# An FNet block with a gated MLP in fp32: the first product of the sequence transform made by seven smaller ones for two chunks at once, and operands of the MLP split in pairs

## The chip, the core and the metric

The kernel runs on one core of one Trainium2 chip. The metric is device time in microseconds (us), the median of three runs. Lower is better. Engines: PE is TensorE (matmul; PEld its weight loads), DVE is VectorE, ACT is ScalarE, POOL is GpSimd, SP issues most of the loads.

## The reference

`x` is 2048 x 512 in fp32. Cut to what matters:

```
xn = layernorm(x)                                  # 2048 x 512
a  = xn @ dft_hid_re.T ;  b = xn @ dft_hid_im.T    # transform along the hidden axis
s  = dft_seq_re @ a - dft_seq_im @ b               # transform along the sequence, 2048 x 2048
g  = silu( (sigmoid(xn @ w_gate) * (xn @ w_up)) @ w_down )   # 512 -> 1792 -> 512
out = x + s * g
```

## The kernel before, in words

**Arithmetic.** Every fp32 matmul is made of three. An operand is split into a high part, a copy rounded to `fp32r` by ACT, and a low part, the rest, subtracted by DVE (`split`, line 370). `mm3` (line 374) issues high x high, high x low and low x high into one PSUM bank. A tile in SBUF is called `page` whatever it holds, and a matmul is 128x128 weights by 512 columns unless a row says otherwise. PSUM has eight banks: `ga`, `ua`, `gb`, `ub`, `gc`, `uc` and two of `pd`.

**Three stages.** First the gated MLP: 14 blocks, two halves `h` of the sequence by seven groups `g` of 256 hidden columns. Then the sequence transform, which is done first of the two transforms and on `xn` itself: `dft_seq_re` and `dft_seq_im` times `xn`, in four chunks of 512 columns. Last the hidden transform, silu and the product. All three use the scheme of Strassen and Winograd: a 2 x 2 block product by seven block products instead of eight, named 1 to 7, of which four have sums or differences of blocks as operands. DVE makes these sums, in fp32, before the split.

**The sequence transform.** `Chunk` (line 1090) is one chunk of 512 output columns. Each of its products runs in four steps `pp` of 12 matmuls, so 48 matmuls a product. The first output block of a chunk is product 1 + product 2; the others build on product 1. Product 2 is not run by `Chunk`. `Inner` (line 1194) makes it for two chunks (`one`, `two`) together, with the scheme applied once more: seven inner products of 2 steps x 6 matmuls, 84 matmuls for both chunks. Its left operands (`inner_a`, line 1025) are made and split once while the MLP runs, stored to DRAM (`i_part`), and loaded again for each pair (`Kept`, line 1058). Its right operands (`inner_b`, line 1071) are loaded from `c_re`; four of seven are sums. `Inner.done` gives each finished bank to a chunk, and `Chunk.give` copies or adds it into the page `u1` that becomes the first output block. Product 1 seeds or stays in the banks `ga`/`ua` (`gb`/`ub` for chunks 2 and 3) in which products 6, 7 and 4 are then accumulated.

**The order of the work.** `PLAN` says for each chunk in which order its steps and those of `Inner` come (digits for `Chunk`, letters a to g for the inner products 1 to 7). Nothing is issued while the Python code runs through this: every call is recorded in `program`, and `emit` (line 319) issues the recorded instructions in the sequence of numbers in `ORDER`. Each engine then takes its own instructions strictly in that order; PE waits for a low part that DVE has not made yet, and DVE waits for a high part that ACT has not made. `HOMES` gives each new page its place in SBUF, so a load also waits for the last reader of that place.

**The MLP's operands.** `w_operands` (line 582) loads a block's weights and makes seven split operands of 128 x 512 (`Parts`, line 406). `Seven` (line 685) does the same for the seven operands of the down projection. Each is one ACT copy and one DVE subtraction. `BLOCKS` is the order of the 14 blocks; where two neighbours share a group `g`, the second uses the operands of the first again.

Of the kernel before, what the change touches and what calls it, by code (L numbers as in the profile page):

```python
# [9 lines left out]
F32 = mybir.dt.float32  # L10
# [5 lines left out]
P = 128  # L16
# [17 lines left out]
0-1 15 2 16 72 5 20 31 3-4 21 6 19 7 29 9 22 11 73 8 23 32 13 74 10 24 26 33 25 17 53 36 12 27 30 108 28 176  # L34
37 34 38 211 39 50 40 14 48 18 41-42 49 43 70 44 54 35 51 71 52 45 47 46 64 60 65 57 56 61-63 80 55 68-69 79
66 81 67 75-76 59 97-98 58 89 77-78 99 82 100 84 90 85 83 86-87 102 88 91 101 92 96 93-94 103 109-110 105
405 95 111-112 117 220 118-119 113 120 125 350 126 121 123-124 106 131 127-129 114 122 130 135 139 115 143
140-142 104 147 133 148 116 144 150-151 154 177 145-146 156-157 149 152 136 153 164 406 158 137 159-160 201
155 161-162 134 138 163 168 179 165 169 181 170 180 166 171-175 202 167 185-189 206 190 204 191-192 203
193-194 182 195 230 212 183 196 207-208 199 132 200 107 219 209-210 235 218 215-216 197-198 217 221 254 222  # L40
213-214 231 225-226 205 227-228 233 223-224 237-238 232 245 241 246 255 236 242 229 256 239-240 385 247 244
248 178 259 234 260 264 257-258 243 261-262 363 267 266 268-269 249 270 265 271-272 251 364 273-274 345
275-276 279 252 280 286-287 285 288-289 250 290-294 263 295 298-301 253 281-282 277 284 278 304 302 305 283
296-297 308 313-314 310 303 306-307 311 317-318 315 424 316 325 319 312 320 329-330 321-322 326-327 333-334
331-332 337 341 346 338 323 365 324 335-336 328 339 348 340 351-353 347 428 354-356 367 369-370 342 371-373
349 374-375 381 376-378 383 366 379-380 387-388 382 389 384 390 343 391-393 399 394 368 395-396 344 397-398
357 401 400 358-360 407 386 450 361 449 362 403 409 402 475 410-411 451 412 408 413 476 414-415 425 416 421
417-419 429 423 420 430 427 431 499 432-433 422 434-436 404 442 437-438 426 439 452 440-441 466 453-455 501
456 443 457-459 446 495 479-480 444 481 467 482 445 483 497 447 484-485 471 486 502 487-488 491 489-490 468
460 448 461-463 493 464 469 465 492 503-505 477 506 472 507-508 473 509 515 510-511 478 512-514 517 540 516  # L50
541 498 542 526 519 527 496 528 522 529-530 518 681 531 543 470 544 546 545 560 538 554 561-563 594 552
564-565 520 532 688 533-534 474 524 535-537 550 547 572 553 573 647 548 574-575 500 549 576-577 184 309 566
578 567-568 539 579 569-570 558 571 598 580 584-585 686 523 586 581 635 582 595 559 583 596 610 589 611 591
612 597 613 587 551 614 599 615 555 588 600 616-617 593 494 618 601 619-620 592 602 621 525 663 521 622
664-665 603 624 633 625-626 557 627-628 590 629 608 666-667 606 623 668 649-650 556 631 607 651-652 630 634
653-655 632 661 656-657 604 658 669 659-660 670 609 672-673 645 674 671 636 675 678 676 640 677 692 662 693
605 694 679 695-696 637 641 648 697 638 708 682 709 642 639 710 680 698 704 643 699-700 690 701 706 702-703
711 646 705 712-713 733 707 715 734-736 714 683 737-738 718 716 720 739-741 717 689 742-743 731 744 644 747
719 748 687 749-751 729 725 752 775 753 776 730 777 887 778 684 732 779 754 780 685 756 721 757 691 722 727
758-759 728 762 760 723 761 781 745 726 763 782-783 804 746 784 1004 764 785-786 768 787 765 788 755 789 766  # L60
773 790 772 791 769 792 815 797 816 793 774 817-818 794 819 767 820 795 770 823-824 799 825 771 826-827 805
828 798 832 801 830 833-835 829 796 836-837 821 831 806 809-810 822 811 803 812 807 813-814 800 857-859 839
808 860-861 847 862 851 838 852 802 853 849 854 840 855 961 856 842 928 865-866 863 867 848 868 891 869-870
844 871 893-894 874 895 864 896-897 872 878 898 909 905 910 875 841 911 876 912 882 913 850 873 914-915 899
843 900 885 901 724 902 907 916 903-904 918 888 877 906 919-921 1003 908 922-923 937 924 879 845 938 880 939
935 940 892 881 941 925 942-943 883 927 944-945 929 946 889 886 930 947-949 951 917 952-953 890 933 954 957
955 926 884 956 970 960 846 971 950 972 958 934 973-974 962 964 975 959 963 976 968 977-978 966 931 979 1010
980 932 981 999 982-983 936 984-985 988 986 965 987 990 989 967 991-992 1002 993 996 994 969 995 1023 1000
997 1024-1026 1021 1001 998 1027 1005 1028 1017 1037-1038 1036 1006 1039 1011 1007 1029-1030 1019 1031 1012
1032-1033 1022 1034 1043 1040-1041 1014 1042 1046 1044 1047 1018 1016 1048 1035 1049 1013 1050 1062 1051  # L70
1020 1066 1052 1015 1067-1068 1058 1069-1070 1055 1071 1053 1072-1073 1060 1054 1074-1075 1064 1056
1076-1077 1009 1080-1081 1078 1082 1059 1083 1008 1084 1079 1085 1092 1098 1086 1099-1100 1057 1096
1101-1102 1061 1103-1104 1110 1105 1063 1106 1045 1107 1087 1108 1065 1109 1088 1114 1111 1115-1117 1089
1120 1118-1119 1123 1121 1124 1090 1125 1137-1138 1129 1091 1139-1140 1094 1141 1093 1142 1209 1126-1127
1097 1128 1143 1095 1130 1144-1146 1112 1147-1149 1113 1132 1150-1151 1135 1152 1133 1153-1155 1166 1136
1167 1156 1168 1131 1169 1157 1170-1171 1162 1172 1122 1158 1173-1174 1164 1175 1159 1176 1163 1177
1180-1181 1160 1182 1165 1213 1186 1214-1215 1161 1216-1218 1178 1183-1184 1179 1185 1189 1187 1190 1199
1191 1134 1200 1192 1188 1195 1193 1207 1194 1219 1208 1196 1220-1222 1198 1197 1223-1224 1201 1230-1231
1225 1232 1202 1227 1211 1228 1203 1229 1244-1246 1204 1226 1247-1248 1266 1249 1205 1250-1251 1233 1206
1252-1253 1234 1254 1210 1255 1240 1256 1235 1257 1212 1269 1258 1237 1270 1259-1260 1242 1261 1277 1236  # L80
1265 1278-1279 1238 1280 1263 1281-1282 1243 1283 1262 1284-1285 1239 1267 1264 1286-1287 1271 1241
1288-1289 1273 1290 1268 1291-1292 1295 1293 1272 1294 1306 1274 1296 1307-1309 1275 1299 1310-1311
1320-1321 1302 1322 1276 1312 1298 1313-1314 1304 1315-1316 1300 1317-1318 1323-1324 1319 1325 1337 1303
1327 1338-1339 1301 1340 1326 1341-1342 1305 1343 1349 1344 1297 1345 1329 1346 1331 1347-1348 1353 1350
1354 1332 1355-1356 1359 1333 1357-1358 1369 1360 1370 1334 1371-1372 1367 1351 1373-1374 1335 1375-1377
1336 1378-1379 1330 1380-1382 1352 1383 1362 1384-1385 1361 1363 1386 1396 1388 1397 1364 1398-1399 1394
1400 1368 1401 1390 1402 1392 1403-1404 1366 1405-1407 1410-1411 1391 1412-1413 1416 1414 1395 1415 1431
1458 1408 1700 1432-1433 1427 1365 1434 1393 1435 1417 1409 1436-1437 1387 1438 1420 1439 1421 1440 1443
1389 1441-1442 1419 1445-1446 1328 1447 1422 1448 1451 1449-1450 1423 1462 1452 1463-1464 1425 1465 1429
1466-1467 1424 1468-1469 1483 1457 1470-1472 1455 1428 1473-1474 1444 1475 1454 1476 1460 1477 1430  # L90
1478-1479 1485 1493-1494 1481 1495 1456 1496 1480 1497-1498 1461 1487 1499-1501 1459 1489 1502-1503 1418
1514 1488 1504-1505 1518 1506 1486 1507 1453 1508 1491 1490 1509-1510 1522 1482 1523 1511 1492 1912
1524-1525 1512 1426 1526-1527 1520 1528 1515 1529 1484 1530-1534 1536 1516 1537-1539 1542 1540-1541 1519
1550 1548 1551 1517 1552 1535 1553-1554 1545 1521 1555-1556 1543 1557 1546 1558-1559 1562 1560 1547 1561
1566 1563 1567-1569 1549 1572 1570-1571 1664 1583 1579 1584-1585 1564 1586-1587 1513 1573 1588 1565 1699
1589 1574 1590 1575 1544 1591 1577 1592-1593 1576 1594-1595 1581 1596 1580 1597-1600 1604 1614 1582 1615
1601 1616-1619 1606 1622 1605 1623-1624 1608 1607 1628 1609-1613 1625 1620 1626-1627 1647 1632 1629 1648
1578 1649-1650 1602 1651-1652 1631 1603 1655 1621 1656 1634 1657 1641 1633 1642-1643 1635 1639 1644-1645
# [1434 lines left out]
```

## Time and profile before

| | |
|---|---|
| median of three runs | 795.08 us (794.29 to 796.54) |
| profiled execution, its device time | 795.25 us |
| span of its profile, first to last instruction | 793.4 us |
| matmuls, PE busy | 3512 (of 3514 issued), 785.5 us |
| DVE | 933 instructions, 716.4 us |
| ACT | 850 instructions, 540.8 us |
| DMA | 173.69 MB, mean 219 GB/s |

An engine's busy time is the time in which at least one of its instructions runs. Instructions of one engine overlap a little at their ends, so the pace of an engine is the distance from one start to the next, and not the duration that a row gives. The stages in the span: the MLP to about 401 us, the sequence transform to about 712 us, then the hidden transform; on DVE and ACT they overlap at the borders.

### The profile page before, as it was taken

What the parts mean: (1) busy time and instruction counts of PE and PEld (TensorE: products, weight loads), DVE (VectorE), ACT (ScalarE), POOL (GpSimd) and SP (SyncE); (2) the same over time, 40 slices, a digit from 0 to 9 for tenths busy, and PEclk for the clock granted to TensorE, in tenths of its full rate; (3) what the DMA queues carried; (4) which work ended last, traced back from release to release, by engine and by line L of the source; (5) the groups of instructions that cost most, each with busy time, mean ns of one, the idle gap of its engine ahead of it and who ended that gap; (6) DMA issues with size and microseconds to landing.
All of it is one profiled execution on the core that took longest, in us unless ns stands there. A gap on an engine that the chain in (4) does not pass through costs nothing.

```text
span 793.4 us, 10135 instructions
## 1 busy us (share of the span) xinstructions
PE 785.5 (99%) x3512; PEld 650.1 (82%) x3512; DVE 716.4 (90%) x933; ACT 540.8 (68%) x850; POOL 127.1 (16%) x174
## 2 busy tenths in 40 slices
PE   8999999999999999999999999999999999999997
PEld 7888887888888888888888888888888888888886
DVE  7999998899979988889898997999987899988986
ACT  5679998879867977877987756554544545457361
POOL 3002442212212322112110101010100000010102
PEclk9999999999999999999999999999999999999999
DMA  8223999969859899999998779359938479569427
GB/s 341 83 81 126 236 198 235 242 151 212 166 137 234 241 231 256 259 203 230 233 309 241 179 280 309 135 159 338 375 142 323 173 282 353 214 244 344 75 54 132
DMA packets 50035, 173.69 MB, mean 219 GB/s; under 512 B 5568, under 2 KB 5824, under 8 KB 49984
## 3 DMA queue, kind: packets, MB, share of 16 engines
q0 software_dynamic: 20160, 69.75, 40.0%
q1 hardware_dynamic: 29744, 103.23, 36.5%
q8 instruction: 27, 0.44, 0.2%
q14 instruction: 24, 0.20, 0.1%
q10 hardware_dynamic: 80, 0.07, 0.0%
HBM read 106.43 MB, written 70.27 MB: 223 GB/s over the span
## 4 chain that ended last, share of the span: by engine, by line
PE 95%; DMA 3%; DVE 1%; ACT 0%; POOL 0%; issue 0%; SPq 0%; DVEq 0%; ACTq 0%; POOLq 0%
PE pd L328 17%; PE ga L328 17%; PE ua L328 16%; PE gc L328 11%; PE uc L328 11%; PE gb L328 11%; PE ub L328 11%; DMA page<-in_w_gu_dram 2%; DMA g_part<-page 1%; DVE page L328 1%; ACT page L328 0%; POOL moments L328 0%; SPq L328 0%; POOL shifts L328 0%; DVE moments L328 0%
## 5 line engine op out<-in xcount | busy, mean ns | idle before, releaser
L328 DVE TENSOR_TENSOR page<-page 128x1024 fp32r<-128x1024 f32 (+5 forms) x756 | 629.5, 891 | 54.8 <-ACT page L328 45.3
L328 ACT ACTIVATE page<-page 128x512 fp32r<-128x512 f32 (+3 forms) x452 | 351.9, 824 | 138.5 <-DVE page L328 113.4
L328 PE MATMUL pd<-page 128*128 128x512 f32 x624 | 159.2, 390 | 0.3 <-ACT page L328 0.2
L328 PE MATMUL ga<-page 128*128 128x512 f32 (+1 forms) x606 | 156.5, 387 | 0.0
L328 PE MATMUL ua<-page 128*128 128x512 f32 (+1 forms) x594 | 154.0, 387 | 1.7 <-ACT page L328 1.7
L328 PEld LDWEIGHTS pd<-page 128*128 128x128 f32 x624 | 116.8, 188 | 25.6 <-ACT page L328 1.3
L328 PEld LDWEIGHTS ga<-page 128*128 128x128 f32 x606 | 113.1, 188 | 23.5 <-ACT page L328 0.2
L328 PEld LDWEIGHTS ua<-page 128*128 128x128 f32 x594 | 110.9, 188 | 24.8 <-ACT page L328 1.9
L328 POOL DMA_DIRECT2D g_part<-page x84 | 70.7, 887 | 316.0 <-ACT page L328 292.9
L328 ACT ACTIVATE page<-pd 128x512 f32<-128x512 f32 (+2 forms) x161 | 89.8, 576 | 38.7 <-PE pd L328 28.3
L328 PE MATMUL uc<-page 128*128 128x512 f32 (+1 forms) x420 | 110.1, 383 | 0.0
L328 PE MATMUL gc<-page 128*128 128x512 f32 (+1 forms) x420 | 109.9, 383 | 0.0
L328 PE MATMUL gb<-page 128*128 128x512 f32 (+1 forms) x420 | 109.0, 380 | 0.0
L328 PE MATMUL ub<-page 128*128 128x512 f32 (+1 forms) x396 | 105.5, 386 | 0.0
L328 PEld LDWEIGHTS uc<-page 128*128 128x128 f32 x420 | 78.0, 188 | 15.7 <-DVE page L328 0.2
L328 PEld LDWEIGHTS gc<-page 128*128 128x128 f32 x420 | 77.8, 188 | 15.7 <-ACT page L328 0.2
L328 PEld LDWEIGHTS gb<-page 128*128 128x128 f32 x420 | 76.9, 188 | 15.4 <-ACT gb L328 0.4
L328 PEld LDWEIGHTS ub<-page 128*128 128x128 f32 x396 | 73.7, 188 | 15.0 <-ACT ub L328 0.2
L328 ACT ACTIVATE page<-ga 128x512 f32<-128x512 f32 x51 | 30.5, 598 | 12.9 <-PE ga L328 12.8
L328 POOL DMA_DIRECT2D f_part<-page x16 | 8.7, 547 | 178.8 <-DVE page L328 165.6
L328 ACT ACTIVATE page<-gb 128x512 f32<-128x512 f32 x32 | 19.1, 598 | 20.0 <-PE gb L328 20.0
L328 ACT ACTIVATE page<-ua 128x512 f32<-128x512 f32 x36 | 21.6, 600 | 8.8 <-PE ua L328 8.3
(59 smaller groups left out, 245.5 us busy)
## 6 DMA issues: line engine op xcount, KB each, us to landing
g_part<-page POOLq DMA_DIRECT2D x84, 512.0 KB, 7.5
page<-in_c_re_dram SPq DMA_DIRECT2D x49, 512.0 KB, 5.9
page<-in_c_im_dram SPq DMA_DIRECT2D x33, 512.0 KB, 7.3
page<-in_w_gu_dram SPq DMA_DIRECT2D x26, 512.0 KB, 7.0
f_part<-page POOLq DMA_DIRECT2D x16, 512.0 KB, 7.6
page<-f_part SPq DMA_DIRECT2D x16, 512.0 KB, 5.4
page<-i_part SPq DMA_DIRECT2D x14, 512.0 KB, 5.1
page<-in_w_down_dram SPq DMA_DIRECT2D x13, 512.0 KB, 5.3
```

The source lines that it names most:

```text
L328: f(*map(found, a), **{n: found(v) for n, v in k.items()})
```

## The change

1. `Inner` now makes product 1 too, from the even blocks of 128 rows of `xn` and `c_re` (`j` = 0; product 2 takes the odd ones, `j` = 1). `PLAN` has capital letters for the inner products of product 1 and has no digits 1 or 2. Both go through `give` into `u1`; the banks of product 6 are seeded from `u1` (`Chunk.run`).
2. For this `inner_a`, `i_part`, `Kept` and `inner_b` exist twice.
3. `twins`: two operands that lie in one page are split by one ACT copy and one DVE subtraction of 128 x 1024 in the place of two of 128 x 512. The MLP's weights are split in three pairs and one single, the operands of the down projection too.
4. `BLOCKS` has the block (1, 5) moved behind (1, 6), so that two groups' weights are used by both halves without being loaded and made again; `shared` keeps them.
5. `ORDER` and `HOMES` are new as a whole.

The instructions that each program issues, counted by engine and shape (only the shapes whose number differs):

```
                                       before  after
PE   matmul 128x512 on pages             3360    3336     (ga -48, ua -48, ub -12, pd +84)
DVE  page<-page 128x1024                 328     427
DVE  page<-page 128x512                  352     191
DVE  page<-page 128x256                   76      94
DVE  page<-page and a bank, 128x512       28      32
ACT  page<-page 128x1024                 213     296
ACT  page<-page 128x512                  225      68
ACT  page<-page 128x256                   14      28
ACT  with a bank, 128x512 (those changed) 295    305
POOL store to i_part                       7      14
SP   load of i_part                       14      28
SP   load of c_re                         49      64
SP   load of w_gu and w_down              39      36
```

The core of the diff:

```diff
-BLOCKS = (*((0, g) for g in range(7)), (1, 6), *((1, g) for g in range(6)))
+BLOCKS = (*((0, g) for g in range(7)), (1, 6), (1, 5), *((1, g) for g in range(5)))
-0-1 15 2 16 72 5 20 31 3-4 21 6 19 7 29 9 22 11 73 8 23 32 13 74 10 24 26 33 25 17 53 36 12 27 30 108 28 176
...
+5565-5568 5572-5573 5569 5574-5579 5570 5580-5583 5571 5584-5587
...
+    def twins(loads, src, names, n):
+        def make():
+            v, pair = src(), (page([2, n]), page([2, n]))
+            split(*pair, v)
+            return pair
+        both = Value(loads, make)
+        return {k: Value(loads, lambda i=i: tuple(t[:, i] for t in both.get())) for i, k in enumerate(names)}
...
-        w = {k: Parts(loads, s, [4 * P], joint=True) for k, s in src.items()}
+        w = {
+            **twins(loads, loads[0].load, (1, 2), 4 * P),
+            **twins(loads, lambda: (s1.get(), s2.get(), two[0].get())[2], (5, 6), 4 * P),
+            **twins(loads, lambda: (s3.get(), s4.get(), two[1].get())[2], (7, 3), 4 * P),
+            4: Parts(loads, raw(1, 1), [4 * P], joint=True),
+        }
...
-            self.h = {k: Parts([], v, [SB], joint=True) for k, v in src.items()}
+            self.h = {
+                **twins([], lambda: (b11(), t1.get(), self.s[1])[2], (1, 5), SB),
+                **twins([], lambda: (b22(), t2.get(), self.s[3])[2], (3, 6), SB),
+                **twins([], lambda: (b21(), t4.get(), self.s[4])[2], (2, 4), SB),
+                7: Parts([], t3.get, [SB], joint=True),
+            }
...
     PLAN = (
-        "1111555566a6a633337777b4b444",
-        "e11e1f1f5c555c66663g3g777733d4d444",
-        "111155556666aa7777b44b44e333ef3f",
-        "1ccg1g1d1555d56666337777334444",
+        "AA5FFBB5GGEE5DDCC56666333377774444",
+        "5a5a5b5b66e66e33f33f77c77c4g44g4dd",
+        "AA5FFBB5GGEE5DDCC56666333377774444",
+        "5a5a5b5b66e66e33f33f77c77c4g44g4dd",
     )
...
             ch = CHAIN[k]
-            if k in FIRST and pp == 0:
+            if k in (5, 6) and pp == 0:
                 for d in range(2):
                     self.ps[ch, d] = bank("gu"[d] + (self.letter if ch == "a" else ch))
+                    if k == 6:
+                        nc.scalar.activation(self.ps[ch, d], self.s["u1"][:, d, :], AF.Copy)
...
-        inner_a([n + i for i in (-43, -39, -39, -38, -37, -33, -27, -20, -12, -10, 1)])
+        inner_a([n + i for i in range(-42, -20, 2)], 1)
+        inner_a([n + i for i in range(-41, -19, 2)], 0)
```

**PE where the sequence transform begins.** The rows below are PE's, in its order, `bank<-page` with the shape and how many follow one another; `pd`, and `gb`/`ub` before, are still the MLP's. Before, at the hand-over from product 1 of chunk 0 (banks `ga` and `ua`) to its product 5 (`gc` and `uc`):

```order
L328 MATMUL ga<-page 128x512 x3
L328 MATMUL ua<-page 128x512 x3
L328 MATMUL pd<-page 128x512 x6
L328 MATMUL gc<-page 128x512 x3
L328 MATMUL uc<-page 128x512 x3
```

Now, with the inner products in `gb` and `ub`, product 5 between them, and product 6 (`ga`) last:

```order
L331 MATMUL ub<-page 128x512 x12
L331 MATMUL gc<-page 128x512 x3
L331 MATMUL gb<-page 128x512 x12
L331 MATMUL gc<-page 128x512 x3
L331 MATMUL ub<-page 128x512 x12
L331 MATMUL uc<-page 128x512 x3
L331 MATMUL gc<-page 128x512 x3
L331 MATMUL pd<-page 128x512 x3
L331 MATMUL gc<-page 128x512 x3
L331 MATMUL uc<-page 128x512 x3
L331 MATMUL pd<-page 128x512 x3
L331 MATMUL ga<-page 128x512 x3
```

The 48 matmuls of product 1 are gone from `ga` and `ua`; 12 at a time stand in one bank instead, and 18 matmuls lie between the last of them and product 6.

**DVE in the second half of the sequence transform.** The rows are DVE's, in its order: `page<-page 128x1024` is a sum of two blocks or a low part, rows with a bank are results taken out of PSUM. Before, where chunk 1 ends and chunk 2 begins:

```order
L328 TENSOR_TENSOR page<-page 128x1024 x8
L328 TENSOR_TENSOR page<-ua,page 128x512
L328 TENSOR_TENSOR page<-ga,page 128x512
L328 TENSOR_TENSOR page<-page 128x1024 x3
L328 TENSOR_TENSOR page<-page,gc 128x512
L328 TENSOR_TENSOR page<-page 128x1024 x7
L328 TENSOR_TENSOR page<-page,gb 128x512
L328 TENSOR_TENSOR page<-page 128x1024 x4
L328 TENSOR_TENSOR page<-page,uc 128x512
L328 TENSOR_TENSOR page<-page 128x1024 x33
```

Now, in the same part of the program:

```order
L331 TENSOR_TENSOR page<-page 128x1024 x9
L331 TENSOR_TENSOR page<-page,pd 128x512
L331 TENSOR_TENSOR page<-page 128x1024 x33
L331 TENSOR_TENSOR page<-page,gc 128x512
L331 TENSOR_TENSOR page<-page 128x1024 x3
L331 TENSOR_TENSOR page<-page,uc 128x512
L331 TENSOR_TENSOR page<-gb,page 128x512
L331 TENSOR_TENSOR page<-ub,page 128x512
L331 TENSOR_TENSOR page<-page 128x1024 x7
L331 TENSOR_TENSOR page<-page,pd 128x512
L331 TENSOR_TENSOR page<-page 128x1024 x14
```

The kinds of work are the same; the stretches of wide instructions between two results are longer. Between the 2209th and the 2738th instruction of PE, 530 matmuls, a part that I call the dense stretch (in both programs it leads from chunk 1 into chunk 2), counted in the written order of all engines, the program before has 87 wide and 12 narrow instructions for DVE, 68 for ACT and 43 loads for SP; the changed one 101 wide and 11 narrow for DVE, 81 for ACT and 57 loads.

More of the change, by code (lines that the diff above doesn't have):

```diff
@@ L39 @@
[L39 to L43, printed above, removed]
@@ L984, in step @@
                 nc.gpsimd.dma_start(to, v)
-        for i, v in zip({diffs: (1, 3, 0, 0), sums: (0, 0, 3, 1)}[make], blocks):
+        for i, v in zip({diffs: (1, 3, 0, 0)}.get(make, (0, 0, 3, 1)), blocks):
             sooner(at[i] - ahead, v.load)
@@ L1069, in fnet_glu_kernel, with inner_b, behind @@
         get = load
-    def inner_b(pair):
+    def inner_b(pair, j):
         b = {}
         for i in range(2):
-            b11, b12, b21, b22 = (Load(c_re[c, 1, 2 * q + i], [2, SB]) for q in range(2) for c in pair)
-            t1 = Value([b11, b12], onto(b11.load, b12.load, SUB, nc.vector, True))
-            t3 = Value([b12, b22], onto(b12.load, b22.load, SUB, nc.vector, True))
-            t2 = Value([b22], onto(t1.get, b22.load, SUB, nc.vector, True))
-            t4 = Value([b21], onto(t2.get, b21.load, SUB, nc.vector, True))
+            b11, b12, b21, b22 = (Load(c_re[c, j, 2 * q + i], [2, SB]) for q in range(2) for c in pair)
+            def behind(k, i, make):
+                return lambda: (b[k, i].get(), make())[1]
+            t1 = Value([b11, b12], behind(1, i, onto(b11.load, b12.load, SUB, nc.vector, True)))
+            t3 = Value([b12, b22], lambda t1=t1, make=onto(b12.load, b22.load, SUB, nc.vector, True): (t1.get(), make())[1])
+            t2 = Value([b22], lambda t1=t1, b22=b22: combine(page([2, SB], F32), b22.load(), t1.get(), SUB))
+            t4 = Value([b21], behind(6, i, onto(t2.get, b21.load, SUB, nc.vector, True)))
             for k, v in {1: b11, 2: b21, 3: b22}.items():
@@ L1141, in done @@
         def done(self, k):
-            if k == 1:
-                if "2" not in PLAN[self.tc]:
-                    for d in range(2):
-                        self.give(d, self.ps["a", d])
-                else:
-                    for d in range(2):
-                        self.ps["b", d] = bank("gu"[d] + "ba"[self.letter == "b"])
-                        nc.scalar.activation(self.ps["b", d], self.ps["a", d], AF.Copy)
-            elif k == 2:
-                self.made[0] = self.snap("u1", "b")
-                self.put(0)
-            elif k == 5:
+            if k == 5:
                 self.snap("u5", "c")
@@ L1174, in run @@
                     ws = [t[:, o, d * P : (d + 1) * P] for t in wv]
-                    first = k in FIRST and pp == e == 0
-                    mm3(self.ps[ch, d], ws, [t[:, e, :] for t in xv], first, pp == 3 and e == 1, go_on=k not in FIRST)
+                    first = k == 5 and pp == e == 0
+                    mm3(self.ps[ch, d], ws, [t[:, e, :] for t in xv], first, pp == 3 and e == 1, go_on=k != 5)
             if pp == 3:
@@ L1420, in fnet_glu_kernel @@
     x_operands(1)
-    job = last = None
+    job, shared = None, {}
     ahead = []
     for h, g in BLOCKS:
-        made = g == last
+        made = h and g in shared
         if not made:
-            w, wd, last = w_operands(g), Down(g), g
+            shared[g] = w_operands(g), Down(g)
+        w, wd = shared[g]
+        if h or g < 5:
+            del shared[g]
         new = Seven(h, wd, made)
```

534 lines of the change are left out of this document (270 added, 264 removed).

## The prediction

> **What bounds the kernel now.** I read the page from the top: the busy times, the slices, then the chain that ended last.
>
> ```profile
> span 793.4 us, 10135 instructions
> PE 785.5 (99%) x3512; PEld 650.1 (82%) x3512; DVE 716.4 (90%) x933; ACT 540.8 (68%) x850; POOL 127.1 (16%) x174
> ...
> PE   8999999999999999999999999999999999999997
> ...
> DVE  7999998899979988889898997999987899988986
> ...
> PEclk9999999999999999999999999999999999999999
> ...
> PE 95%; DMA 3%; DVE 1%; ACT 0%; POOL 0%; issue 0%; SPq 0%; DVEq 0%; ACTq 0%; POOLq 0%
> ```
>
> The reader sees one engine that never rests: PE in every slice but the first and the last, at full clock, and 95% of the chain. DVE is second with 90%. So a matmul taken away is worth its whole pace, as long as nothing else makes PE wait. Next the stretches between fixed times (columns: time, PE, PEld, DVE, ACT and POOL busy with their instructions, clock, DMA share, GB/s), and all that PE waited for:
>
> ```profile
> 20.00:120.00 100.00, 100.00 (x451) 82.44 (x451) 98.55 (x160) 84.67 (x151) 25.28 (x33) 1.00 0.54 146
> 132.00:402.00 270.00, 269.79 (x1191) 222.86 (x1190) 243.95 (x384) 220.01 (x400) 55.85 (x72) 1.00 0.91 217
> 496.00:616.00 120.00, 120.00 (x531) 99.10 (x530) 108.79 (x100) 59.16 (x68) 8.23 (x13) 1.00 0.70 245
> 616.00:712.00 96.00, 96.00 (x425) 79.48 (x424) 87.04 (x82) 50.07 (x56) 4.42 (x8) 1.00 0.69 250
> 780.00:793.40 13.40, 9.03 (x52) 7.75 (x50) 7.78 (x12) 0.00 (x0) 2.95 (x3) 1.00 0.91 175
> ```
>
> ```profile
> PE ua L328 <- ACT page L328: 1.7, 1, 1.7
> PE gb L328 <- DVE page L328: 1.4, 1, 1.4
> PE pd L328 <- ACT page L328: 0.2, 1, 0.2
> ```
>
> Two things matter. From 20 to 120 us DVE was busy 98.55 of 100 us and PE lost nothing, so a nearly full DVE is not by itself a stall. And PE's idle time, 793.4 - 785.5 = 7.9 us, lies at the two ends (4.4 us in the last row, 3.1 us in the first two waits): there is nothing inside to win but matmuls.
>
> **The matmuls removed.** The chain in order of time (start, duration, what) gives the pace:
>
> ```profile
> 712.70 5.44 PE pd L328 x24
> 723.58 5.44 PE pd L328 x24
> ```
>
> 24 matmuls take 5.44 us, 0.2267 us each; the 390 ns that a row gives as one matmul's duration overlap with the next. Product 1 by `Chunk` is 48 matmuls, 96 for two chunks; by `Inner` 84. Two pairs save 2 x 12 = 24 matmuls of the same shape, 5.44 us of PE.
>
> **DVE's price.** DVE's rows in order of time (start, duration), where it does not rest:
>
> ```profile
> 62.37 0.68 DVE L328 TENSOR_TENSOR page<-page,uc 128x512 f32<-128x512 f32 x1
> 62.97 0.69 DVE L328 TENSOR_TENSOR page<-page 128x512 f32<-128x512 f32 x1
> 63.57 0.68 DVE L328 TENSOR_TENSOR page<-page,gc 128x512 f32<-128x512 f32 x1
> ...
> 399.21 1.23 DVE L328 TENSOR_TENSOR page<-page 128x1024 fp32r<-128x1024 f32 x1
> 400.36 0.68 DVE L328 TENSOR_TENSOR page<-page,ua 128x512 f32<-128x512 f32 x1
> 400.95 1.22 DVE L328 TENSOR_TENSOR page<-page 128x1024 fp32r<-128x1024 f32 x1
> 402.09 0.68 DVE L328 TENSOR_TENSOR page<-page,gc 128x512 f32<-128x512 f32 x1
> ```
>
> From start to start a narrow one (512) costs 0.60 us and a wide one (1024) 1.15 and 1.14; I take 1.14. For 128x256 I take the duration, as an upper end:
>
> ```profile
> L328 DVE TENSOR_TENSOR page<-page 128x256 f32<-128x256 f32 x62 | 25.3, 420 | 0.2
> L328 ACT ACTIVATE page<-page 128x1024 fp32r<-128x1024 f32 x205 | 209.9, 1056 | 125.7 <-DVE page L328 102.4 <-PE ub L328 6.9 <-issue 5.1
> L328 ACT ACTIVATE page<-page 128x512 fp32r<-128x512 f32 x197 | 118.5, 630 | 5.9 <-DVE page L328 4.1 <-DMA page<-in_w_gu_dram 1.8
> L328 ACT ACTIVATE page<-page 128x256 fp32r<-128x256 f32 x14 | 5.5, 419 | 0.0
> ```
>
> Over the program DVE gets 99 wide more (+112.9), 161 narrow fewer (-96.6), 18 of 256 more (+7.6) and 4 out of banks more (+2.4): +26.3 us, from 716.4 to about 743 in a span of about 790, 94%. ACT by the durations above: 83 x 1.056 - 157 x 0.63 + 14 x 0.42 + 10 x 0.63 (those with a bank) = +0.9 us. ACT has a third of the span free; its change is at nothing.
>
> It must be read by stage. Pairing saves 2 x 0.60 - 1.14 = 0.06 us of DVE a pair, and two groups fewer to make save their sums and splits; these lie in the MLP. The new operands of product 1 are DVE work in the sequence transform. In the dense stretch of the written order (530 matmuls, 530 x 0.2267 = 120.2 us), DVE had 87 wide and 12 narrow, 87 x 1.14 + 12 x 0.60 = 106.4 us. The trace's row 496 to 616 is that part with 108.79 us, so the sum is good to about 2%. Now it has 101 x 1.14 + 11 x 0.60 = 121.7 us for 120.2 us of matmuls. DVE falls 1.5 us behind there. The low parts are written into the list only about as far ahead of their first matmul as the instruction itself lasts (the nearest 5 matmuls, 1.1 us), so I let all of 1.5 us show as waits of PE. In no other part of that length does the sum pass PE's.
>
> DVE's own waits come on top, if it still has them:
>
> ```profile
> DVE page L328 <- ACT page L328: 6.5, 8, 1.5
> DVE page L328 <- DMA w_part<-page: 1.2, 1, 1.2
> DVE page L328 <- DMA f_part<-page: 0.7, 1, 0.7
> ```
>
> These are its waits from 496 to 616 us (total, times, longest). They cost nothing while DVE has 11.2 us free there. The bounds for what stays are 0 and all of 11.2 us. I take 0 plus the noise, by the list: before, in the dense stretch 17 of 55 low parts were the next DVE instruction after the ACT copy that they need, now 3 of 61; those with four or more DVE instructions between went from 10 to 30. DVE is not sent to a high part that is only being made.
>
> **The other parts.** The seed of product 6: the last inner bank of chunk 0 must be added into `u1` by DVE (0.68) and copied into two banks by ACT (2 x 0.60) before `ga`; 1.9 us, against 18 matmuls between, 4.1 us. At nothing; behind a DVE queue more than 2 us late it would show, and that is the 1.5 us again. The pairs of the MLP make the first operand wait for the second's sum, one DVE instruction, 0.60 us; in the first two rows of stretches PE lost 0.21 us in all, with DVE as full as it was, so nothing, with 0 to 5 us as bounds (eight such waits). The MLP's second half loses three weight loads and the splits of two groups: PE is the bound there, so nothing.
>
> **Queues.** SP gets 29 loads more and 3 fewer, POOL 7 stores more: 33 x 0.52 MB = 17.3 MB, a tenth.
>
> ```profile
> page<-in_c_re_dram SPq DMA_DIRECT2D x49, 512.0 KB, 5.9
> ...
> page<-i_part SPq DMA_DIRECT2D x14, 512.0 KB, 5.1
> ```
>
> In the dense stretch SP issues 57 loads in the place of 43. With POOL's issues, 13 before and 14 now, the DMA share of 0.70 becomes 0.70 x 71/56 = 0.89. From 132 to 402 us it was 0.91 and PE lost 0.21 of 270 us. So hidden; bounds 0 and some 4 us.
>
> **The sum.** Against the profiled execution: 795.25 - 5.44 + 1.5 = 791.3 us. That execution is 0.17 above the median shown, so 791.2 us for the median, -0.5%. A change under 0.3% (2.4 us) can't be told from none.
>
> **The rivals.**
> - *No stall at all.* DVE's lead at the start of the dense stretch absorbs the 1.5 us, as the lead from 20 to 120 us did. Then 795.1 - 5.4 = 789.7 us. Against it: those 120 us are over 100% full. 22 in 100.
> - *DVE keeps its waits for ACT* (the case of the other sign). Place: the dense stretch. If the 6.5 us in 8 waits stay, DVE needs 121.7 + 6.5 = 128.2 us there, PE waits 8.0, and the time is 797.6; with all 11.2 us 802.3. It takes the whole gain from 5.44 us of stall on and makes the kernel slower from 7.8. For it: ACT itself waits for DVE's sums, so a late DVE can make itself wait. Against it: the list's distances. 16 in 100, 12 of them slower.
> - *Loads come late.* Three or four loads of `c_re` or `i_part` landing a microsecond late, as `w_part` did with 1.2: +4 us, 795.2. 11 in 100, 3 slower.
> - *The pairs cost what they save*: waits in the MLP of up to 5 us, 796. 6 in 100, no change.
>
> - *A full queue does not overlap.* If each DVE instruction cost its whole duration, 1.22 and 0.68 us by the rows, the dense stretch would need 101 x 1.22 + 11 x 0.68 = 130.7 us, a stall of 10.5 in the place of 1.5, and the time would be 795.1 - 5.4 + 10.5 = 800.2. Against it: the rows show it the other way; the instruction of 62.37 us ends at 63.05, and its follower began at 62.97. 3 in 100. [...]
>
> [...]
>
> That PE's work does not shrink is excluded: the count of instructions is 24 lower at equal shapes.
>
> **How the numbers follow.** The forecast has 42 in 100, its own range 790 to 792.7. Faster: 42 + 22 less 2 for its edge, 0.62. Same: 2 + 4 + 8 + 6 and 1 of the rule, 0.21. Slower: 12 + 3 + 2, 0.17. For the range I go below the case without a stall by what the median shown leaves open (789.7 - 0.9), and up into the second rival, past its 797.6 to 798.5; outside stay its worst cases and the rule.
>
> **What would show it.** PE has 3490 instructions and the pace of 24 in 5.44 us. The waits of PE name DVE pages with 1 to 3 us in all, around 500 to 620 us, where DVE is busy over 97%. DVE's total is 735 to 745 us, its waits for ACT in that stretch under 2 us. I am wrong if PE's waits there pass 5 us, or if a stage shows waits that had none (PE on ACT at product 6, SP's loads on the MLP's side), or if the first 20 us, whose order is also new, move by more than 1 us.

## The result: slower by 1%, and where the profile after shows it

| | before | changed |
|---|---|---|
| median (range) | 795.42 us (794.29 to 796.54, 4 runs) | 804.2 us (802.23 to 807.1, 4 runs) |
| ratio, 95% interval | | 1.0113 [1.0078, 1.0149] |
| profiled execution, span | 795.25, 793.4 us | 807.1, 805.3 us |

I had forecast 791.2 us, between 788.8 and 798.5. The page of the changed kernel, the same lines as before:

```profile
span 805.3 us, 10034 instructions
PE 786.8 (98%) x3488; PEld 642.9 (80%) x3488; DVE 735.6 (91%) x893; ACT 546.6 (68%) x800; POOL 132.5 (16%) x181
...
PE   8999999898999999999999999999999999999997
...
PE 74%; DMA 11%; issue 6%; DVE 5%; ACT 1%; POOL 1%; SPq 0%; DVEq 0%; ACTq 0%; POOLq 0%
```

The 24 matmuls are gone (3488 records for 3512; the programs themselves issue these numbers, not two more as stated ahead), and DVE's total of 735.6 us is at the lower edge of the forecast 735 to 745. But the chain is no longer PE alone: a quarter of it are DMAs, DVE and issue. The stretches between fixed times say where. The first row is of the kernel before, which the prediction did not show; the other four are of the changed one:

```profile
402.00:496.00 94.00, 94.00 (x416) 77.70 (x415) 84.56 (x88) 63.31 (x82) 9.54 (x13) 1.00 0.84 257
```
```profile
132.00:402.00 270.00, 265.17 (x1155) 214.93 (x1154) 236.66 (x334) 209.02 (x345) 60.00 (x79) 1.00 0.92 227
402.00:496.00 94.00, 92.80 (x405) 75.40 (x404) 89.63 (x91) 67.21 (x87) 7.71 (x10) 1.00 0.88 270
496.00:616.00 120.00, 116.64 (x507) 93.94 (x506) 112.88 (x105) 67.26 (x80) 9.97 (x15) 1.00 0.85 295
616.00:712.00 96.00, 96.00 (x425) 79.27 (x424) 93.32 (x88) 53.74 (x60) 3.71 (x7) 1.00 0.85 319
```

Read the number behind PE's busy time. Matmuls overlap (one of 128x512 lasts 0.39 us by its row, at a pace of 0.2267), so the busy time hides a small gap; the count does not. In the MLP (132 to 402 us) PE started 1155 matmuls where it had started 1191: 36 x 0.2267 = 8.2 us lost. In the two stretches of the sequence transform it is 11 and 24 matmuls, 2.5 and 5.4 us. After 616 us nothing is lost. The budget: 795.25 - 5.44 + 16.1 = 805.9 us, and the end adds 1.4: from the end of the last matmul to the end of the span it is 5.8 us now and was 4.4. The sum is 807.3, measured 807.1. I use this count of matmuls as the measure below. At 0.2267 us a full stretch of 120 us holds 529, and the kernel before counts 531, so a count is good to about two matmuls, 0.5 us.

The fixed times cut the two programs at different places, so I also follow the dense stretch by its own matmuls, the 2209th to the 2738th of PE. First before, then now, with DVE's waits for a load and for ACT in it now:

```profile
495.70:615.70 120.00, 120.00 (x530) 99.12 (x529) 108.79 (x100) 58.86 (x68) 8.23 (x13) 1.00 0.70 245
```
```profile
507.70:631.40 123.70, 121.92 (x531) 98.59 (x530) 120.61 (x111) 69.90 (x82) 9.10 (x14) 1.00 0.85 296
```
```profile
DVE page L331 <- DMA page<-in_c_im_dram: 1.2, 1, 1.2
DVE page L331 <- ACT page L331: 0.5, 1, 0.5
```

From its first start to its last it took 120.0 us and takes 123.7: 3.6 us more, where the forecast had 1.5. DVE is idle 3.1 us in it. Ahead of it, from 402 us to its begin at 507.7, the distances between PE's starts exceed the pace by 4.2 us in sum (0.1 before). So the 16.1 us divide into about 8.2 in the MLP, 4.2 ahead of the dense stretch and 3.6 in it.

What PE waited for in the whole changed kernel (total, times, longest):

```profile
PE pd L331 <- ACT page L331: 3.9, 4, 1.6
PE pd L331 <- DVE page L331: 1.8, 3, 0.7
PE ub L331 <- ACT ub L331: 1.8, 2, 1.6
```

**The wait in the MLP followed back.** Rows in order of time (start, duration, what; in brackets the idle time before and what ended it), of POOL, SP, DVE, ACT and PE:

```profile
125.23 2.62 POOL L331 DMA_DIRECT2D g_part<-page  x3 [6.79 <-ACT page L331]
126.89 1.70 POOL L331 DMA_DIRECT2D m_part<-moments  x1
```
```profile
140.67 2.13 SPq L331 DMA_DIRECT2D page<-m_part  x2
```
```profile
148.94 6.63 DVE L331 TENSOR_TENSOR page<-page 128x1024 f32<-128x1024 f32 x8 [4.88 <-DMA page<-m_part]
```
```profile
152.73 1.06 ACT L331 ACTIVATE page<-page 128x1024 fp32r<-128x1024 f32 x1 [3.88 <-DVE page L331]
```
```profile
154.32 0.96 PE L331 MATMUL pd<-page 128*128 128x512 f32 x3 [1.16 <-ACT page L331]
```

`m_part` (4 KB, factors of the layernorm) goes to DRAM by POOL behind three stores of 512 KB, issued in the 1.7 us before it, and is loaded again by SP. SP waited 12.4 us for it; before, the longest such wait in that part was 2.8 us. DVE stands 4.88 us at the multiplication with that load. The sums of the down projection stand behind it, ACT's split waits for them, the copies that empty the `pd` banks stand behind the split, and PE waits for a bank. No link of this is a matter of how long an instruction takes.

```profile
SPq L331 <- DMA m_part<-moments: 12.4, 1, 12.4
```
```profile
SPq L328 <- DMA m_part<-moments: 2.8, 1, 2.8
```

The kernel before has a like pair of DMAs at nearly the same time:

```profile
126.69 1.06 POOL L328 DMA_DIRECT2D m_part<-moments  x1
```
```profile
142.33 0.33 SPq L328 DMA_DIRECT2D page<-m_part  x1
```

By the records that store landed after 10.1 us and that load after 11.2; now it is 13.6 and 8.2, about the same in sum. What differs is the room in the written order. Before, 79 matmuls of PE (17.9 us) stand between the store and the load and 61 (13.8 us) between the load and DVE's first use of it; now 49 (11.1 us) and 22 (5.0 us). Neither is enough for what the DMAs take.

**The longest wait in the sequence transform** is of the same make:

```profile
496.32 1.04 SPq L331 DMA_DIRECT2D page<-in_c_re_dram  x2
```
```profile
502.76 2.00 ACT L331 ACTIVATE page<-page 128x1024 fp32r<-128x1024 f32 x2 [5.64 <-DMA page<-in_c_re_dram]
504.67 0.58 ACT L331 ACTIVATE ub<-gb 128x512 f32<-128x512 f32 x1
```
```profile
503.85 3.50 DVE L331 TENSOR_TENSOR page<-page 128x1024 fp32r<-128x1024 f32 x3 [2.49 <-ACT page L331]
```
```profile
505.30 0.97 PE L331 MATMUL ub<-page 128*128 128x512 f32 x3 [1.58 <-ACT ub L331]
```

A load of `c_re` is issued at 496.3 us, when the last matmul has left its place (by the records no other of the 54 places was free then; two that came free at 493.3 and 493.5 went to other pages), and its page is there for ACT 6.4 us later. ACT stands 5.6 us before it, with the copy of an inner bank behind the split; DVE stands 2.5. This wait lies ahead of the dense stretch.

From the records I also worked out how many of the 54 places are held (from the first write of a page to the end of its last reader or the landing of its store). From 132 to 285 us it was 47.5 in the mean and is 51.8; from 285 to 402, 48.2 and 50.9; from 496 to 616, 52.1 and 52.3. So the MLP lost most of its spare places, while the sequence transform had few before. The number alone does not make the loss: in the first two of the rearranged kernels below it is within 0.6 of the changed kernel's in both parts of the MLP, and PE loses 1.4 to 1.6 us there.

Three theories follow. P: places and queues; a load or copy waits for a place or a DMA, and holds up all behind it on its engine. D: DVE is too full in the sequence transform. T: the pairs themselves make the first operand late.

### The profile page after: what moved, and what is told of

It is laid out like the page before. It is cut to its first block, busy times and chain, and to the rows that moved or that the text cites. A ratio compares the mean times of both kernels' runs of the same rounds, so it can differ in the third digit from the quotient of the medians.

```text
span 805.3 us, 10034 instructions
## 1 busy us (share of the span) xinstructions
PE 786.8 (98%) x3488; PEld 642.9 (80%) x3488; DVE 735.6 (91%) x893; ACT 546.6 (68%) x800; POOL 132.5 (16%) x181
## 4 chain that ended last, share of the span: by engine, by line
PE 74%; DMA 11%; issue 6%; DVE 5%; ACT 1%; POOL 1%; SPq 0%; DVEq 0%; ACTq 0%; POOLq 0%
PE pd L331 16%; PE ga L331 11%; PE ua L331 10%; PE gb L331 9%; PE ub L331 9%; PE uc L331 9%; PE gc L331 9%; DVE page L331 5%; DMA g_part<-page 3%; DMA f_part<-page 2%; DMA page<-in_c_re_dram 2%; DMA page<-i_part 2%; DMA page<-in_w_gu_dram 1%; ACT page L331 1%; DMA page<-in_c_im_dram 1%
## 5 line engine op out<-in xcount | busy, mean ns | idle before, releaser
L331 DVE TENSOR_TENSOR page<-page 128x1024 f32<-128x1024 f32 (+5 forms) x712 | 646.6, 970 | 35.3 <-ACT page L331 17.2
L331 ACT ACTIVATE page<-page 128x1024 fp32r<-128x1024 f32 (+4 forms) x392 | 350.6, 935 | 133.5 <-DVE page L331 89.0
L331 PE MATMUL pd<-page 128*128 128x512 f32 x708 | 185.0, 392 | 5.1 <-ACT page L331 3.9
L331 PEld LDWEIGHTS pd<-page 128*128 128x128 f32 x708 | 131.6, 188 | 37.2 <-ACT page L331 8.4
L331 PE MATMUL ga<-page 128*128 128x512 f32 (+1 forms) x558 | 142.0, 387 | 0.5 <-DVE page L331 0.5
L331 PE MATMUL ua<-page 128*128 128x512 f32 (+1 forms) x546 | 140.1, 388 | 1.1 <-DVE page L331 0.6
L331 PEld LDWEIGHTS ga<-page 128*128 128x128 f32 x558 | 103.9, 188 | 22.8 <-issue 0.9
L331 PEld LDWEIGHTS ua<-page 128*128 128x128 f32 x546 | 101.6, 188 | 23.8 <-DVE page L331 2.0
L331 PE MATMUL ub<-page 128*128 128x512 f32 (+1 forms) x384 | 99.2, 387 | 2.1 <-ACT ub L331 1.8
L331 DVE TENSOR_TENSOR page<-page,gc 128x512 f32<-128x512 f32 x34 | 23.2, 683 | 8.8 <-PE gc L331 6.6
L331 ACT ACTIVATE page<-ua 128x512 f32<-128x512 f32 x34 | 20.4, 599 | 12.9 <-PE ua L331 11.2
```

Source lines behind the costliest of these rows:

```text
L331: f(*map(found, a), **{n: found(v) for n, v in k.items()})
```

## The experiments

Matmuls that PE started in the three stretches, and what is lost against the kernel before (differences x 0.2267 us):

| kernel | 132-402 | 402-496 | 496-616 | lost, us | median, us | ratio to before, 95% |
|---|---|---|---|---|---|---|
| before | 1191 | 416 | 531 | | 795.1 to 795.4 | |
| changed | 1155 | 405 | 507 | 16.1 | 804.2 | 1.0113 [1.0078, 1.0149] |
| changed, once more | 1155 | 407 | 508 | 15.4 | 800.96 | 1.0073 [1.0047, 1.0098] |
| new places, all | 1168 | 405 | 517 | 10.9 | 808.95 | 1.0161 [1.0139, 1.0183] |
| new places, MLP | 1167 | 409 | 511 | 11.6 | 802.0 | 1.0082 [1.0069, 1.0095] |
| new places, sequence | 1160 | 400 | 515 | 14.3 | 810.79 | 1.0199 [1.0177, 1.0221] |
| half the low parts | 1166 | 408 | 523 | 9.3 | 799.49 | 1.0048 [1.0034, 1.0062] |
| small stores | 1188 | 406 | 511 | 7.5 | 797.56 | 1.0027 [1.0018, 1.0037] |
| rearranged, first | 1184 | 406 | 519 | 6.6 | 799.12 | 1.0044 [1.0029, 1.006] |
| rearranged, second | 1185 | 404 | 522 | 6.1 | 798.14 | 1.0043 [1.0029, 1.0058] |
| second, half the low parts | 1185 | 410 | 525 | 4.1 | 794.81 | 0.9995 [0.9986, 1.0004] |
| rearranged, third | 1182 | 413 | 518 | 5.7 | 796.79 | 1.0017 [1.0008, 1.0025] |
| third, nine sums on POOL | 1181 | 412 | 476 | 15.6 | 806.18 | 1.0141 [1.0128, 1.0155] |

The same executions, with the dense stretch followed by its 530 matmuls (excess: by how much the distances between PE's starts pass the pace, in sum):

| kernel | excess from 402 us to the dense stretch, us | dense stretch, us | DVE busy in it, us |
|---|---|---|---|
| before | 0.1 | 120.0 | 108.8 |
| changed | 4.2 | 123.7 | 120.6 |
| changed, once more | 3.7 | 123.0 | 120.5 |
| half the low parts | 3.7 | 120.0 | 99.9 |
| small stores | 2.2 | 124.2 | 120.5 |
| rearranged, first | 2.8 | 121.9 | 120.6 |
| rearranged, second | 2.7 | 121.6 | 120.5 |
| second, half the low parts | 1.3 | 121.2 | 99.6 |
| rearranged, third | 0.5 | 122.7 | 120.9 |
| third, nine sums on POOL | 0.8 | 132.2 | 128.4 |

All of this is of one profiled execution of each kernel. That of the changed kernel was the slowest of its runs, both times, and that of the first two rearranged kernels and of the new places for all pages the fastest (795.96, 795.91 and 804.64 us). So the profiles show more difference than the medians do; read the medians for what a variant is worth, and the profiles for where it loses. The new places for all pages and for the sequence transform also lose 12 and 16 matmuls (2.7 and 3.6 us) from 616 to 712 us, which the first table leaves out.

The runs fall into three sets, each on one chip beside the kernel before: new places and half the low parts; the changed kernel once more to the second rearrangement; the last three. Between sets only the ratios can be compared. The runs of the changed kernel spread wider than those of before: 797.34 to 805.13 in the second set, against 794.26 to 797.67.

**The changed kernel once more**, the measure for the runs beside it.

> The changed kernel itself once more, as the measure for the runs beside it. Every theory: 804.2, between 802 and 807.

800.96 us, a little under the expected bounds, and still slower than before.

**New places, three runs.** Only the letters of `HOMES`:

```diff
 HOMES = (
...
-    "zlsjPpGWwZMhXemutykrxYEOcCiDLl1HPqXsvhrNKMuZOdgTiBuNKhqHuTKrBAGQJIVjpWrhOGTZLCvRug1ZpOzEvT1KRhjFuSrv"
+    "zlsjPpGWwZMhcXekumytYOEClDri1LhxHPvscNqMKCktZdrBTgkMxKNPkBxAgqQGIVpWJAjKQBD1tZRcrk1hJQzDRE1cKFWjrRkZ"
...
```

> Same instructions in the same order as the changed kernel; only the letters of HOMES are chosen anew, from 100 us on, so that a page takes, where it can, a place that has long been free (54 places as before). In the changed kernel PE's starts leave 8.8 us of gaps from 80 to 285 us and 8.0 us from 396 to 592 us. Theory P (places: the change keeps more pages alive, a place is handed on as soon as its last reader or its store to DRAM is done, and a load or a copy that waits for it holds up all that stands behind it on its engine): most of these gaps go, 804.2 - 10 = 794, between 791 and 797. Theory D (DVE is too full in the sequence transform, as the prediction's stall had it, only more): the 8.0 us there stay, and no more than the MLP's part can go. Theory T (the pairs themselves make the first operand late): the MLP's 8.8 us stay. D and T together: 804, within 1.5.

> The new places only for pages first used before 392 us (the MLP); later pages keep their places as in the changed kernel, up to a renaming of the letters. P: of the 8.8 us of gaps in the MLP 5 to 8 go, 796 to 799.5. T (the pairs' own delays): within 1.5 of 804.

> The new places only for pages first used after 392 us (the sequence and the hidden transform). P: 3 to 6 of the 8.0 us of gaps there go, 798 to 801.5. D: DVE's work is the same, so within 1.5 of 804.

The MLP's part went the way of P, but not as far as it forecast: the loss in that stretch fell from 8.2 to 5.4 us (from 80 to 285 us, the gaps that P spoke of fell by 4.9 of 8.8 us, for 5 to 8 expected), and of PE's 3.9 us of waits for ACT at `pd` 0.8 us are left. From 80 to 392 us:

```profile
PE ub L331 <- ACT ub L331: 0.9, 1, 0.9
PE pd L331 <- ACT page L331: 0.8, 1, 0.8
PE uc L331 <- DVE page L331: 0.5, 1, 0.5
PE ua L331 <- DVE page L331: 0.2, 1, 0.2
```

As a time, 802.0 lies between P's range and T's, and its ratio of 1.0082 can't be told from the changed kernel's own, 1.0113 and 1.0073. The two others failed all theories: 810.79 and 808.95, slower than the changed kernel. The profile of the one with the sequence's places shows new waits, one of 3.2 us, from 392 us on:

```profile
PE uc L331 <- DVE page L331: 3.4, 2, 3.2
PE ua L331 <- DVE page L331: 1.8, 5, 0.5
PE pd L331 <- DMA page<-i_part: 0.8, 1, 0.8
```

My rule gave a page that is not loaded the place that had come free last before its turn, so it had little slack against a DMA that lands late. By the records, from 392 to 616 us in the run with the sequence's places, a page that is not loaded is begun 1.05 us in the median after the last use of its place, and 55 of 250 within 0.3 us; in the changed kernel it is 1.52 us and 30 of 252. That is no evidence for D, but it shows what places weigh: the same instructions in the same order, 802.0 and 810.79 us in one set.

**Half the low parts** (DVE's work in the sequence transform):

```diff
+        if isinstance(v, Ref) and id(v.cell) in half:
+            v = first(v)
...
+            if n in HALF:
+                a = [v[:, :1] for v in a]
```

> Places as in the changed kernel. 68 of the low parts of 128x1024 that DVE makes between 443 and 598 us are made only for their first 512 columns, and the matmuls take that half for both: part of the result is left out. DVE gets 68 x (1.14 - 0.60) = 36.7 us free there, a quarter of that stretch. D: all 8.0 us of PE's gaps there go, 796, between 795 and 798. P: DVE itself waits there for loads and for ACT (6.4 us from 480 to 520 us); only those gaps go whose last link is a low part that DVE reached late, 0.41 + 0.43 + 0.52 + 0.55 + 0.69 = 2.6 us: 801.6, between 800 and 803.

799.49, between the two theories. DVE's total is 702.1 us, 33.5 less, and PE's loss from 402 to 616 us falls from 7.9 to 3.6 us:

```profile
402.00:496.00 94.00, 92.67 (x408) 75.96 (x407) 79.08 (x90) 67.75 (x88) 7.72 (x10) 1.00 0.87 273
496.00:616.00 120.00, 118.41 (x523) 97.71 (x522) 94.69 (x109) 70.85 (x84) 10.00 (x15) 1.00 0.86 303
```
```profile
PE ub L348 <- ACT ub L348: 2.9, 2, 1.6
```

What is left is one kind of wait (440 to 600 us): ACT's bank copy behind a split that waits for its load, at 454 and 502 us. Both lie ahead of the dense stretch, where the excess stays (4.2 and 3.7 us). In the dense stretch nothing is lost any more:

```profile
505.00:625.00 120.00, 120.00 (x531) 99.32 (x530) 99.96 (x111) 69.59 (x82) 9.13 (x14) 1.00 0.86 305
```

So the two theories hold at two places: the loss in the dense stretch hangs on DVE's time, as D has it, and the loss ahead of it on loads, as P has it.

**Small stores** in the MLP:

```diff
+            if n in SMALL:
+                a = [v[:, :1, :P] for v in map(found, a)]
```

> The changed kernel, but the 37 stores that add a page to g_part between 101 and 283 us move 64 KB (128 of 512 columns of one half) in the place of 512 KB: part of the MLP's result is left out. DVE's, ACT's and PE's work is the same, and the pairs too. In the changed kernel such a store takes 7.0 us in the median and up to 12.4 from issue to landing, and holds its page's place as long; the store of 4 KB to m_part that stands behind four of them took 12 us. Theory P (places and queues behind DMAs): PE's 8.8 us of gaps from 80 to 285 us fall to 3 or less, the sequence transform keeps its 8.0: 798, between 796 and 800. Theory T (the pairs themselves make the first operand late): the gaps stay, within 1.5 of the changed kernel beside it.

797.56, 3.4 us under the changed kernel beside it. The loss in the MLP fell from 8.2 to 0.7 us, no wait of PE is left there from 80 to 392 us, and SP's wait for `m_part` is 2.5 us:

```profile
132.00:402.00 270.00, 269.95 (x1188) 222.22 (x1188) 244.13 (x344) 215.06 (x354) 60.10 (x79) 1.00 0.70 182
```
```profile
SPq L339 <- DMA m_part<-moments: 2.5, 1, 2.5
```

The pairs are all there, with DVE and ACT busy 244 and 215 us in that stretch. T falls: the pairs' own delays cost under 1 us. What cost 8 us is waiting for DMAs. (By the medians small stores are worth 3.4 us and not 7.5, as the changed kernel's profiled execution was its slowest.) This run makes the stores themselves faster, the rest of the traffic lighter (share 0.70) and the places free sooner, all at once; which of the three counts it does not tell.

**The same instructions rearranged.** No work is left out. The moves were found by replaying the trace's durations in each engine's order, with landings of DMAs that vary as they do in the trace. The first lines of the third (698 goes ahead, 630 back):

```diff
-617 656-657 653 627 658-659 644 670 626 671 622 661 672-673 660 674-675 618 629 676 662 677-679 682 680 630
-681 686 683 687-689 692 684 690-691 685 726 509 693 727 697 728 698 694 729-730 709 731-732 712 623 713 695
+617 656-657 653 627 658-659 644 670 626 671 622 661 672-673 660 674-675 698 618 629 676 662 677-679 682
+680-681 686 683 687-689 692 684 690-691 685 726 509 693 727 697 728 694 729-730 709 731-732 712 623 713 695
...
```

> The same 5588 instructions. 115 of DVE's, ACT's, SP's and POOL's stand up to a few positions earlier or later in their engine's own order, and 269 of 1095 pages have another of the 54 places, so that waits for loads, stores and places have more slack; PE's order is untouched. P: most of PE's gaps after 80 us go, 16.8 us to 7 or less, in the sequence transform too (8.0 to 4 or less): 794, between 790 and 798. Theory D (DVE has 121.7 us of work for 120.2 us of matmuls in the dense stretch, and no order helps): the gaps from 392 to 600 us stay above 6 us, and the time is 796 if all of the MLP's go, 800 to 804 if they don't.

> A second rearrangement of the same kind, found from another start: 143 instructions moved in their engine's own order, 207 pages in other places. P: as for the first, 794, between 790 and 798, and the two within 3 us of each other. D: 796 to 804, with more than 6 us of PE's gaps from 392 to 600 us.

> A third rearrangement of the same 5588 instructions, carried on from the first: 179 moved in their engine's own order, 559 pages in other places, PE's order untouched. P: PE's gaps after 80 us, 7.1 and 6.4 us in the first two, fall below 6, and the time to 796.5, between 794 and 798.5. If order and places have given what they can, 798 to 799, like the first two.

799.12, 798.14 and 796.79. The first two are 2 and 3 us under the changed kernel beside them and miss P's range (790 to 798), while their times lie in D's (796 to 804); the third's time is in P's range, but PE's gaps after 80 us are 6.5 us there, not below 6. The profile says more than the times about the place. The second one:

```profile
132.00:402.00 270.00, 269.88 (x1185) 221.15 (x1184) 244.76 (x343) 214.99 (x352) 59.83 (x79) 1.00 0.94 231
402.00:496.00 94.00, 92.94 (x404) 75.00 (x403) 87.79 (x87) 66.18 (x85) 7.76 (x10) 1.00 0.87 273
496.00:616.00 120.00, 119.36 (x522) 97.28 (x522) 118.42 (x110) 69.96 (x82) 10.02 (x15) 1.00 0.87 302
```

The MLP loses 1.4 us at full DMA traffic (share 0.94). In the last row DVE is busy 118.42 of 120 us and PE lost 9 matmuls, 2.0 us. The 530 matmuls of the dense stretch take 121.6 us with 120.5 us of DVE's work, where the changed kernel took 123.7 with 120.6: the same work, less waiting. So D as I stated it (no order helps, more than 6 us of gaps) falls in these executions, where the gaps from 392 to 600 us are 4.5 and 4.2 us; they were the fastest of their runs, and where the slower ones lose 2 to 3 us more was not recorded. None of the three is faster than the kernel before.

**The second one with half the low parts** puts the two together:

> The second rearranged kernel (798.1 us; PE's gaps from 392 to 600 us are 4.2 us there, DVE is busy 118.4 of 120 us from 496 to 616) with the same 68 low parts made for half their columns as in the run with half the low parts, so that DVE gets 36.7 us free: part of the result is left out. Theory PD (a late load becomes a wait of PE because a full DVE has no time left to catch up): the 4.2 us fall to 1.5 or less, 795.4, between 794 and 797. Theory P alone (what is left are loads that land late, whatever DVE has to do): 3 us or more of the gaps stay, 798, within 1.

The time, 794.81, is in PD's range:

```profile
402.00:496.00 94.00, 93.32 (x410) 76.34 (x409) 77.72 (x89) 67.29 (x87) 7.77 (x10) 1.00 0.87 277
496.00:616.00 120.00, 119.58 (x525) 97.96 (x526) 97.12 (x109) 69.17 (x82) 10.02 (x15) 1.00 0.87 303
```

The loss from 402 to 616 us falls from 4.8 to 2.7 us. The gaps from 392 to 600 us fall from 4.2 to 2.4 us, between the 1.5 of PD and the 3 of P alone. By the ratios the time falls by 0.5%, some 4 us, so DVE's time counts, with the same loads in the same order. Not all of it need be catching up: DVE is also the last reader of places that loads wait for, and with less work it frees some sooner. Counted in matmuls of PE, the loads issued from 440 to 600 us stand in the median where they stood, but 23 of 69 come 1 to 7 matmuls earlier (4 come later), and SP's waits for DVE there fall from 48.3 to 30.6 us.

**Nine sums on POOL**, an attempt to buy that time without leaving work out:

```diff
+ON_POOL = 3302, 3722, 3780, 3923, 3965, 4001, 4104, 4180, 4236
...
+            if n in ON_POOL:
+                f = pool.tensor_tensor
```

> The third rearrangement with nine of DVE's differences of two pages (128x1024, between 441 and 580 us) computed by POOL, which is busy 10 of 120 us there; nothing is left out. DVE gets 9 x 1.14 = 10.3 us free. PD: PE's gaps from 392 to 600 us are 1 to 2 us smaller than in the third rearrangement alone, and so is the time. No trace of this case shows such an instruction on POOL; if one takes over 4 us, or if DVE stands still beside it, the stores and operands behind it come late: up to 9 x 1.14 = 10 us slower if DVE stands still for as long as DVE itself would have needed.

806.18, 9.4 us slower than without, near the worst case that was expected. POOL's rows, and DVE's wide ones from 440 to 600 us, first of the third rearrangement, then of this run:

```profile
L333 POOL TENSOR_TENSOR page<-page 128x1024 f32<-128x1024 f32 x9 | 24.3, 2696 | 30.1 <-DMA page<-in_c_re_dram 21.8 <-issue 4.2 <-DMA page<-in_c_im_dram 4.2
```
```profile
L328 DVE TENSOR_TENSOR page<-page 128x1024 fp32r<-128x1024 f32 x77 | 91.2, 1220 | 3.1 <-ACT page L328 1.1 <-DMA f_part<-page 1.0 <-PE ga L328 0.4
L328 DVE TENSOR_TENSOR page<-page 128x1024 f32<-128x1024 f32 x48 | 57.0, 1219 | 1.7 <-DMA page<-in_c_re_dram 1.3 <-DMA page<-in_c_im_dram 0.3
```
```profile
L333 DVE TENSOR_TENSOR page<-page 128x1024 fp32r<-128x1024 f32 x72 | 98.0, 1395 | 5.4 <-ACT page L333 2.7 <-DMA f_part<-page 1.1 <-DMA g_part<-page 0.5
L333 DVE TENSOR_TENSOR page<-page 128x1024 f32<-128x1024 f32 x36 | 46.2, 1314 | 1.6 <-DMA page<-in_c_re_dram 1.6
```

DVE's mean rose from 1220 to 1395 and 1314 ns: 72 x 0.175 + 36 x 0.095 = 16.0 us more, for 8 x 1.14 = 9.1 us of work taken away there. By single records the rise sits on eight instructions of 2.5 to 3.7 us, each beside one of the eight POOL instructions of that stretch; all others kept 1.22. Each of the eight ends 1.08 to 1.09 us after the end of its POOL instruction, as if DVE had stood still until POOL was done. One of them, first POOL, then DVE, whose third instruction is the stretched one (it ends at 543.02, POOL at 541.93):

```profile
539.14 2.79 POOL L333 TENSOR_TENSOR page<-page 128x1024 f32<-128x1024 f32 x1 [5.88 <-DMA page<-in_c_re_dram]
```
```profile
537.14 5.88 DVE L333 TENSOR_TENSOR page<-page 128x1024 f32<-128x1024 f32 x3
```

The dense stretch takes 132.2 us in the place of 122.7, which is the whole loss.

## Why the prediction was wrong, by its own steps

- *The matmuls removed, 5.44 us*: right. 3488 records, the pace of 6 in 1.36 us unchanged.
- *DVE's price*: right where it decides. In the dense stretch the sum had 121.7 us of DVE for 120.2 us of matmuls; measured are 120.6 us of DVE, and the rearranged kernels run the 530 matmuls in 121.9, 121.6 and 122.7 us. Over the whole program the sum was too high: +19.2 us where it had +26.3.
- *"The bounds for what stays are 0 and all of 11.2 us. I take 0 plus the noise"*: wrong by 2 us. The dense stretch lost 3.6 us and not 1.5, as DVE was idle 3.1 us in it; with half the low parts the loss there is gone. Only 0.5 us of the 3.1 was for ACT, so the list's distances between ACT and DVE, which I argued from, did hold; the longest wait was for a load (1.2 us). The rival "DVE keeps its waits for ACT" had 8.0 us there, and is wrong in size and root.
- *"In no other part of that length does the sum pass PE's"* and *"So hidden; bounds 0 and some 4 us"* (the loads): the first inference that failed. Between 402 us and the dense stretch, where the sums leave room, 4.2 us are lost, 1.6 of them in one wait behind a load that ACT stood 5.6 us for. I took the DMA share, 0.91 from 132 to 402 us at a loss of 0.21, as the sign of what can be hidden. In the changed kernel the share there is 0.92 and the loss 8.2; rearranged it is 0.94 and 1.4. The share says nothing of how long before its use a load can be issued. That hangs on when a place comes free: by the records, 29 of 36 loads from 132 to 392 us are issued within 0.3 us of it before, and 28 of 33 now.
- *The pairs of the MLP, "so nothing, with 0 to 5 us as bounds"*: the largest miss, 8.2 us. I priced one sum of DVE for a pair. The pairs' own delay is under 1 us (small stores); what I left out are the shorter distances from POOL's store of `m_part` to SP's load and on to its use, four engines' queues behind them, and the places. The rearranged kernels, with all pairs and full stores, lose 1.4 to 2.0 us there. I never looked at the queues of this stage, since its engine sums had not changed.
- *The seed of product 6*: no wait of PE is at that copy. A copy of the same kind between inner banks does wait, behind a late split.
- *What would make me wrong* named one sign that came, a stage with waits that had none (the MLP). The other, over 5 us in the dense stretch, did not come: it was 3.6.
- *A full queue does not overlap* (800.2 us): that its time lies nearer to the measured one than the forecast is luck. Where the changed kernel's DVE does not rest, its wide instructions still start 1.14 us apart at a duration of 1.22: 33 in a row from 594.98 us take 37.70 us. "The rule" in the prediction's sum of the chances is this rival. No run shows DVE's instructions following one another at their whole duration.

Not settled: the 1.4 us at the end of the span; which of the change's parts takes the four places in the MLP (pairs, groups kept for both halves, or the second set of left operands were not tried apart); how the MLP's 8.2 us divide between order and places, as new places alone won 2.8 us and the rearranged kernels changed both; and why the runs spread.

## What to carry to other kernels

Before pricing a change by the engines' sums, follow the DMA queues in every stage whose order changes, also where its work does not: measure in the written order how far each load stands ahead of its use, and behind the store or the last reader that it needs, and compare that with what such DMAs take in the trace. In the changed kernel one late DMA was passed on from queue to queue: SP stood 12.4 us for a store of 4 KB, DVE 4.88 us for the load behind it, ACT 3.88 us for DVE, and PE 1.16 us for ACT. A DMA share of 0.91 went with a loss of 0.2 us from 132 to 402 us and one of 0.92 with a loss of 8.2; ask how early each load's place comes free. A nearly full engine cost nothing where nothing arrived late (before, DVE was busy 98.55 of 100 us and PE lost nothing) and something where loads did (second rearrangement: with DVE busy 97.12 in the place of 118.42 of 120 us, the loss from 402 to 616 us fell from 4.8 to 2.7 us), so its slack is worth pricing as such.

## What the runs showed of the hardware

- DVE's wide instructions took longer beside POOL's: a difference of two 128x1024 pages took POOL 2.4 to 3.3 us (nine, 2.70 us in the mean), and of DVE's instructions of 128x1024, 1.22 us long elsewhere, eight took 2.5 to 3.7 us, each beside one of POOL's, and ended 1.08 to 1.09 us after it. Why they end so late was not shown.
- A store of 4 KB behind three stores of 512 KB on the same queue held its reader for 12.4 us in the changed kernel; with 64 KB in the place of the 512 KB it was 2.5 us. A load of 512 KB took 6.1 us in the median from issue to landing, in the changed kernel:

```profile
page<-in_c_re_dram SPq DMA_DIRECT2D x64, 512.0 KB, 6.1
```
